# One PSUM tile each for the turned last rows of k and of q, in place of one tile that both share

## The chip, the core and the metric

The kernel runs on one core of a Trainium2 chip. Its five engines work side by side: TensorE (PE) multiplies matrices and turns tiles, VectorE (DVE) and ScalarE (ACT) move results out of PSUM and do the elementwise work, GpSimd (POOL) helps with copies and integer sums, and SyncE (SP) issues DMA transfers. The metric is the device time in microseconds (us). The kernel before takes 1052.27 us, the median of 3 runs (1051.37 to 1053.14).

## What is computed

Three parts follow one another: attention with a memory term, a gated layer, and a second gated layer on its output. Batch, heads, rows and depth are 4, 8, 576 and 64; the gated layers have 2304 rows, width 512 and inner width 1536.

```python
def _attn_ref(q, k, v, M_prev, z_prev, beta):
    scores = scale * np.matmul(q, k.transpose(0, 1, 3, 2))
    scores = np.where(causal, -1000000000.0, scores)
    a = np.exp(scores - scores.max(-1, keepdims=True))
    a /= a.sum(-1, keepdims=True) + 1e-09
    local = np.matmul(a, v)
    q_p = phi(q)                       # elu(q) + 1
    mem_out = einsum(q_p, M_prev) / (einsum(q_p, z_prev) + 1e-06)
    return g * mem_out + (1 - g) * local        # g = sigmoid(beta)

def _moe_ref(x, w_gate, w_val, w_out):
    return (sigmoid(x @ w_gate) * (x @ w_val)) @ w_out

def _moe2_ref(x, w_a, w_b, w_out):
    return ((x @ w_a) * (x @ w_b)) @ w_out
```

## The kernel before

Attention works on pairs of heads: 16 pairs, p = 0 to 15. The 576 rows of a pair are cut into five blocks, the first of 64 rows and four of 128. The blocks form two groups, X (0, 2, 3) and Y (1, 4). For each pair PE turns k and q, so that depth lies on the partitions (`turn` for the first 448 columns, CUT, and `turn4` for the last 128), multiplies them (`scores`, L233), and then turns the exponentials and the mixed tiles (`turn_w` at L368, `turn_mix` at L380) and multiplies them with v (`pv`, L398 and L404). DVE takes the maxima of the scores (L262), ACT the exponentials (L267). From pair 9 on (PARTS) the turned k and q are kept as a high and a low part, and a score takes three products.

PE also works on the first gated layer: while the attention of batch 1 and later batches is computed, the gated layer of the batch before runs in single products of three matmuls each (`mm3`, L484 to L486), which the loop places between the steps of attention (step `M`). The weights come in by DMA and are unpacked on the way (L438 to L454, steps `W`). After the attention, the rest of the gated layers runs as one dense stretch of matmuls on PE.

PSUM has eight banks. Four hold the scores (`psa`). A pool of three, `pst`, serves in turn all the turned tiles and the outputs of `pv`: every call of `tp()` takes the next of its three buffers. Up to pair 4 each fourth call takes a fourth bank instead (`psx`); from then on this bank belongs to the gated layer (`psm`). So a tile of `tp()` can be written only when the tile that had the same bank three calls before has been copied out. In one turn of the loop the calls come in a written order (`FIRST`, `FIFTH` and `LATER`): of that order the steps `m0`, `m1`, `mY` (mixed tiles), `wA` (two tiles, one per head), `t4` (`turn4`), and in the next turn `pvX`, `pvY`, `wB` and `wC` matter here. The copies out of the `wA` tiles are made on ACT (L152, names `aw<-tp`, 128x512).

Only the order within some steps is pinned; else the framework places each instruction on its engine by its own estimate of times. So a change of the tiles can move instructions on all engines. The turned last rows of k are copied out by ACT (L176, `kt`), those of q by DVE (L173, `qt`); from pair 9 on both are copied by ACT (L167) and then by DVE (L168).

Of the kernel before, what the change touches and what calls it, by code (L numbers as in the profile page):

```python
# [19 lines left out]
def kernel(  # L20
# [17 lines left out]
    P = 128  # L38
    B, H, S, D = q.shape
# [8 lines left out]
    CUT = 448  # L48
# [105 lines left out]
    def tp():  # L154

        turns[0] += 1
        return (psx if psm is None and turns[0] % 4 == 0 else pst).tile([P, 512], F32, tag="tp", name="tp")


    def put(p, key, src, a, z):  # L160
        if a == 0:
            st[key, p] = at.tile([P, 2, S], F32, tag=f"{key}t", name=f"{key}t")
        t = st[key, p][:, 0, a:z]
        scale = -1.0 / D ** 0.5 if key == "q" else 1.0
        if p >= PARTS:
            h, l = (st[key, p][:, i, a:z].bitcast(F32R) for i in H2)
            act.activation(out=h, in_=src, func=AF.Copy, scale=scale)  # L167
            r = vec.scalar_tensor_tensor(  # L168
                out=l, in0=src, scalar=scale, in1=t, op0=ALU.mult, op1=ALU.subtract
            )  # L170
            return r
        elif key == "q":
            return vec.tensor_scalar(  # L173
                out=t, in0=src, scalar1=scale, scalar2=None, op0=ALU.mult
            )
        return act.activation(out=t, in_=src, func=AF.Copy)  # L176

    def turn1(out, p, key, i):
        src = st[f"{key}n", p][:, i].rearrange("p h d -> p (h d)")
        pe.transpose(out=out, in_=src, identity=ident)  # L180

    def begin():


        idle, tk, tq = tp(), tp(), tp()

        def spin(n):
            for _ in range(n):
                pe.matmul(
                    idle[:, 0:P], lhsT=tws[0], rhs=tws[1], start=True, stop=True,  # L190
                    skip_group_check=True,
                )

        act.activation(out=early, in_=tws[0][:, 0:2], func=AF.Exp)
        spin(5)
        turn1(tk[:, 0:P], 0, "k", 0)
        turn1(tq[:, 0:P], 0, "q", 0)
        spin(4)
        for key, t in (("q", tq), ("k", tk)):
            for i in (1, 2, 3):  # L200
                turn1(t[:, C03[i]:C03[i] + P], 0, key, i)
            st["first", key] = put(0, key, t[:, 0:CUT], 0, CUT)
        turn4(0)
# [5 lines left out]
        put(p, key, t[:, 0:CUT], 0, CUT)  # L209

    def turn4(p):
        t = tp()
        for c, key in enumerate("kq"):
            turn1(t[:, c * P:(c + 1) * P], p, key, 4)
        for c, key in enumerate("kq"):
            put(p, key, t[:, c * P:(c + 1) * P], CUT, S)

    def scores(p, blocks):

# [401 lines left out]
    if True:  # L621
# [89 lines left out]
        def one(step, p):  # L711
# [27 lines left out]
            elif step == "phi1" and new:  # L739
                if not p:  # L740
                    load_z(0)
                phi1(p)
            elif step == "phi2" and new:
                phi2(p)
            elif step == "lv" and new:
                load_v(p)
            elif step == "lz" and nx:
                load_z(nx)
            elif step in ("tk", "tq") and nx:
                turn(nx, step[1])  # L750
            elif step == "t4" and nx:
                turn4(nx)
            elif step in ("m0", "m1", "mY") and old is not None:
                turn_mix(old, step[1])
            elif step == "M":
                M()
            elif step == "Mo" and old is not None:
                M()
            elif step == "S":
                settle()  # L760
            elif step == "sp":
                split(1)
            elif step == "W":
                if p >= 1:
                    for _ in range(1 if p < 4 else 2):
                        w_next()
# [50 lines left out]
    with tc.manual_schedule(engines={mybir.EngineType.PE}):  # L817
# [46 lines left out]
        for c in range(MA):  # L864
            for kind in range(3):
                t = ws[0, c, kind]
# [869 lines left out]
```

## Time and profile before

| | |
|---|---|
| median of 3 runs | 1052.27 us (1051.37 to 1053.14) |
| profiled execution | 1050.67 us |
| its span, first to last instruction | 1048.8 us |
| PE busy | 1026.1 us, 98% |
| DVE busy | 736.2 us, 70% |
| ACT busy | 589.7 us, 56% |
| POOL busy | 188.6 us, 18% |
| mean granted TensorE clock | 0.998 |

The profiled execution's time is 1.9 us over its span, and 1.6 us under the median of the runs. A matmul's busy time overlaps that of the next, so the step from one start to the next is what it costs: a row "x12" in a timeline stands for twelve in a row, with the start of the first. "[0.98 <-PE tp L368]" behind a row says that the engine was idle for 0.98 us before it and that the release came from PE's line 368. The first 120 us, where attention runs alone or with little beside it, have nearly all of PE's idle time up to the end of attention.

### The profile page before, as it was taken

How to read it: one execution, taken by the hardware profiler on the slowest of the kernel's cores; microseconds unless marked ns; L12 is line 12 of the kernel's file. 1: busy time of each engine (PE TensorE's matmuls, PEld its weight loads, DVE VectorE, ACT ScalarE, POOL GpSimd, SP SyncE). 2: the span in 40 equal slices, each digit the busy share in tenths (PEclk: the TensorE clock that was granted, in tenths of full speed). 3: DMA queues.
4: the chain of work that ended last, by engine and by line, in shares of the span. 5: the costliest groups of instructions: out<-in, count | busy, mean ns of one | idle time of the engine just before them, and what ended most of it. 6: DMA issues, size and time to landing. Idle time of an engine off the chain costs nothing.

```text
span 1048.8 us, 17727 instructions
## 1 busy us (share of the span) xinstructions
PE 1026.1 (98%) x6158; PEld 858.6 (82%) x6158; DVE 736.2 (70%) x1590; ACT 589.7 (56%) x1276; POOL 188.6 (18%) x204
## 2 busy tenths in 40 slices
PE   7988999999999999999999999999999999999998
PEld 5656777777878987888888889888888888899998
DVE  6888755665627797765587558686586676898885
ACT  7888867867836556445654335454444545453442
POOL 3544521331211111111211000221121311000000
PEclk9999999999999999999999999999999999999999
DMA  7665434233215424332378754444362575644441
GB/s 174 157 182 159 136 90 127 77 87 85 59 55 172 161 86 145 103 128 80 118 247 300 241 170 161 131 136 136 96 190 91 188 232 183 216 142 146 137 141 61
DMA packets 154697, 150.14 MB, mean 143 GB/s; under 512 B 74608, under 2 KB 112624, under 8 KB 154608
## 3 DMA queue, kind: packets, MB, share of 16 engines
q1 hardware_dynamic: 152560, 148.16, 45.8%
q8 instruction: 48, 0.79, 0.3%
q10 hardware_dynamic: 2048, 0.86, 0.3%
q14 instruction: 41, 0.34, 0.1%
HBM read 103.29 MB, written 45.69 MB: 142 GB/s over the span
## 4 chain that ended last, share of the span: by engine, by line
PE 79%; DVE 7%; ACT 5%; DMA 5%; issue 2%; POOL 1%; SPq 1%; ACTq 0%; DVEq 0%; POOLq 0%
PE gv L486 17%; PE gv L485 17%; PE gv L484 17%; PE gv L1474 10%; PE m L484 3%; PE m L486 3%; PE m L485 3%; PE tp L404 2%; PE sc L233 2%; PE tp L368 2%; ACT s L267 2%; PE tp L398 1%; PE tp L380 1%; ACT aw L152 1%; DMA st<-in_moe_w_b_dram 1%
## 5 line engine op out<-in xcount | busy, mean ns | idle before, releaser
L484 PE MATMUL gv<-xm,w 128*128 128x512 f32 (+1 forms) x752 | 272.4, 362 | 0.5 <-ACT ev L1207 0.4
L486 PE MATMUL gv<-xm,w 128*128 128x512 f32 (+1 forms) x752 | 272.6, 363 | 0.0
L485 PE MATMUL gv<-xm,w 128*128 128x512 f32 (+1 forms) x752 | 272.6, 363 | 0.0
L925 POOL TENSOR_TENSOR wt<-wt,st 128x512 int32<-128x512 int32 x60 | 84.3, 1408 | 496.1 <-DVE wt L921 356.9
L484 PEld LDWEIGHTS gv<-xm,w 128*128 128x128 f32 x752 | 141.4, 188 | 23.8 <-ACT ev L1207 1.3
L485 PEld LDWEIGHTS gv<-xm,w 128*128 128x128 f32 x752 | 141.5, 188 | 22.6
L486 PEld LDWEIGHTS gv<-xm,w 128*128 128x128 f32 x752 | 141.6, 188 | 22.0
L1207 ACT ACTIVATE ev<-gv 128x512 f32<-128x512 f32 (+1 forms) x172 | 93.8, 562 | 76.2 <-PE gv L486 58.0
L1211 DVE TENSOR_TENSOR ev<-gv,ev 128x512 f32<-128x512 f32 x120 | 80.9, 684 | 63.0 <-PE gv L486 31.8
L1474 PE MATMUL gv<-wo,gs 128*128 128x256 f32 x1008 | 120.8, 282 | 0.1
L1474 PEld LDWEIGHTS gv<-wo,gs 128*128 128x128 f32 x1008 | 120.3, 190 | 0.7 <-DVE gs L1447 0.5
L152 ACT ACTIVATE aw<-tp 128x512 f32<-128x512 f32 (+2 forms) x144 | 69.0, 507 | 46.3 <-PE tp L368 32.5
L262 DVE CUSTOM_DVE_ANT_0 s<-sc,mask 128x64 f32<-128x64 f32 (+4 forms) x160 | 69.0, 484 | 21.7 <-PE sc L233 21.6
L915 ACT ACTIVATE wt<-st 128x512 f32<-128x512 f32 x60 | 39.7, 668 | 73.5 <-DMA st<-in_moe_w_out_dram 30.7
L1446 ACT ACTIVATE gs<-ev 128x512 fp32r<-128x512 f32 (+1 forms) x96 | 51.1, 572 | 52.7 <-DMA ev<-gd 25.1
L267 ACT ACTIVATE s<-s,mx 128x320 f32<-128x320 f32 (+3 forms) x128 | 77.3, 607 | 2.7 <-DVE mx L262 2.7
L916 ACT ACTIVATE st<-st 128x512 int32<-128x512 uint32 x60 | 40.2, 669 | 39.5 <-DMA st<-in_moe_w_gate_dram 14.3
L486 PE MATMUL gv<-gs,w 128*128 128x512 f32 (+1 forms) x160 | 59.6, 373 | 0.0
L485 PE MATMUL gv<-gs,w 128*128 128x512 f32 (+1 forms) x160 | 59.4, 371 | 0.0
L233 PE MATMUL sc<-kt,qt 64*128 64x320 f32 (+4 forms) x468 | 55.8, 367 | 3.4 <-DVE mx L262 2.9
L484 PE MATMUL gv<-gs,w 128*128 128x512 f32 (+1 forms) x160 | 58.9, 368 | 0.0
L1447 DVE TENSOR_TENSOR gs<-ev,gs 128x512 fp32r<-128x512 f32 (+1 forms) x96 | 56.0, 617 | 3.3 <-ACT gs L1446 3.2
(159 smaller groups left out, 1825.7 us busy)
## 6 DMA issues: line engine op xcount, KB each, us to landing
gd<-ev SPq DMA_DIRECT2D x80, 256.0 KB
ev<-gd SPq DMA_DIRECT2D x80, 256.0 KB
st<-in_moe_w_out_dram SPq DMA_DIRECT2D x24, 512.0 KB
st<-in_moe_w_gate_dram SPq DMA_DIRECT2D x12, 512.0 KB
st<-in_moe_w_val_dram SPq DMA_DIRECT2D x12, 512.0 KB
st<-in_moe_w_a_dram SPq DMA_DIRECT2D x12, 512.0 KB
st<-in_moe_w_b_dram SPq DMA_DIRECT2D x12, 512.0 KB
x<-rd SPq DMA_DIRECT2D x32, 144.0 KB
```

Of the source, the lines that this page charges most:

```text
L152: act.activation(out=out, in_=src, func=AF.Copy)
L233: st["anchor"] = pe.matmul(scs[e][:, SC0[i] + a:SC0[i] + z], lhsT=x, rhs=y, start=n == 0, stop=n == len(terms) - 1, skip_group_check=True,)
L262: st["pace"] = vec.tensor_tensor_reduce(out=s, in0=scs[e][:, SC0[i]:SC0[i] + w], in1=mask[:, c:c + w], scale=1.0, scalar=BIG, op0=ALU.add, ...
L267: st["apace"] = act.activation(out=o, in_=s, func=AF.Exp, scale=-1.0, bias=mx[:, i:i + 1], accum_out=sms[p % 2][:, i:i + 1, e],)
L484: pe.matmul(o, lhsT=w[:, 0, ws_], rhs=xh, start=first, stop=False, skip_group_check=True)
L485: pe.matmul(o, lhsT=w[:, 0, ws_], rhs=xl, start=False, stop=False, skip_group_check=True)
L486: return pe.matmul(o, lhsT=w[:, 1, ws_], rhs=xh, start=False, stop=last, skip_group_check=True)
L925: pool.tensor_tensor(out=c32, in0=c32, in1=lo, op=ALU.add)
L1207: act.activation(out=t[:, 0:n], in_=src[:, 0:n], func=func)
L1211: st["gate"] = vec.tensor_tensor(out=t, in0=src, in1=t, op=ALU.add)
L1447: vec.tensor_tensor(out=t[:, 1, 0:n], in0=f[:, 0:n], in1=t[:, 0, 0:n].bitcast(F32), op=ALU.subtract,)
L1474: st["gate"] = pe.matmul(o, lhsT=t[:, th, q_], rhs=w[:, wl_, wc:wc + 256], start=first and (ends_ or not r) and not z, stop=last and (ends ...
```

## The change

`turn4` takes two tiles of `tp()` in place of one. Before, the turns of k and of q went side by side into columns 0 to 255 of one tile, and both copies followed. Now k is turned and copied, and then q from a tile of its own.

```diff
     def turn4(p):
-        t = tp()
-        for c, key in enumerate("kq"):
-            turn1(t[:, c * P:(c + 1) * P], p, key, 4)
-        for c, key in enumerate("kq"):
-            put(p, key, t[:, c * P:(c + 1) * P], CUT, S)
+        for key in "kq":
+            t = tp()
+            turn1(t[:, 0:P], p, key, 4)
+            put(p, key, t[:, 0:P], CUT, S)
```

The number of matmuls, copies and transfers is the same; a turn of the loop takes 16 tiles of `tp()` in place of 15. Line numbers below `turn4` are one lower after the change (L232 for L233, L397 for L398).

On PE, around the start of pair 2, the kernel before turns the last rows of pair 2, multiplies the first half of pair 0's output, and only then comes to the scores of pair 2 (`sc`); `kn` and `qn` are the rows of k and q, `aw` the copied tiles:

```order
L180 MATMUL tp<-ident,kn 128x128
L180 MATMUL tp<-ident,qn 128x128
L398 MATMUL tp<-aw,mv 64x320 x2
L404 MATMUL tp<-aw,vn 64x256 x4
L404 MATMUL tp<-aw,vn 64x128 x2
L368 MATMUL tp<-ident,s 128x128 x4
L233 MATMUL sc<-kt,qt 128x64 x2
L233 MATMUL sc<-kt,qt 128x320 x2
L233 MATMUL sc<-kt,qt 128x448 x2
```

The changed kernel has at the same place:

```order
L367 MATMUL tp<-ident,s 128x128 x4
L232 MATMUL sc<-kt,qt 128x64 x2
L232 MATMUL sc<-kt,qt 128x320 x2
L232 MATMUL sc<-kt,qt 128x448 x2
L180 MATMUL tp<-ident,qn 128x128
L397 MATMUL tp<-aw,mv 64x320
L180 MATMUL tp<-ident,kn 128x128
L397 MATMUL tp<-aw,mv 64x320
L403 MATMUL tp<-aw,vn 64x256 x4
L403 MATMUL tp<-aw,vn 64x128 x2
```

The scores have moved ahead of the output matmuls, and the turns of the last rows behind the scores. (The scores of group X don't need the last rows.)

On ACT, in pair 6, `aw` are the copies of the turned exponentials, `sg` is the first sigmoid, `mix` the first exponentials of the pair, and `ACT_TABLE_LOAD` changes the function table. The order before is:

```order
L152 ACTIVATE aw<-tp 128x512
L530 ACT_TABLE_LOAD
L530 ACTIVATE sg<-sg 128x1024
L267 ACT_TABLE_LOAD
L267 ACTIVATE mix,sm_93<-s_1355,mx 128x64
L267 ACTIVATE mix,sm_93<-s_1358,mx 128x64
L152 ACTIVATE aw<-tp 128x512
L453 ACTIVATE w_1340<-wt 128x512
L267 ACTIVATE s,sm_93<-s,mx 128x320
L152 ACTIVATE aw<-tp 128x512
```

And after the change:

```order
L152 ACTIVATE aw<-tp 128x512
L529 ACT_TABLE_LOAD
L529 ACTIVATE sg<-sg 128x1024
L452 ACTIVATE w_1347<-wt 128x512
L152 ACTIVATE aw<-tp 128x512
L176 ACTIVATE kt<-tp 128x128
L266 ACT_TABLE_LOAD
L266 ACTIVATE mix,sm_93<-s_1362,mx 128x64
L266 ACTIVATE mix,sm_93<-s_1365,mx 128x64
```

The last copy of the two `wA` tiles, and that of k's last rows, have moved ahead of the second table load. On DVE a piece earlier, at pair 5, three operations have moved ahead of the first maxima, behind which they stood: the subtraction of a second weight piece (L454), the scaling of the next (L438) and `qp` (L287).

On PE in the later pairs, here where the first half of a pair's output begins at 176.66 us in the trace of before, the order before is:

```order
L180 MATMUL tp<-ident,kn 128x128
L180 MATMUL tp<-ident,qn 128x128
L484 MATMUL m<-xs,w_794 128x512
L485 MATMUL m<-xs,w_794 128x512
L486 MATMUL m<-xs,w_794 128x512
L484 MATMUL m<-xs,w_794 128x512
L485 MATMUL m<-xs,w_794 128x512
L486 MATMUL m<-xs,w_794 128x512
L398 MATMUL tp<-aw,mv 64x320 x2
```

And after the change:

```order
L180 MATMUL tp<-ident,kn 128x128
L483 MATMUL m<-xs,w_798 128x512
L484 MATMUL m<-xs,w_798 128x512
L485 MATMUL m<-xs,w_798 128x512
L483 MATMUL m<-xs,w_798 128x512
L484 MATMUL m<-xs,w_798 128x512
L485 MATMUL m<-xs,w_798 128x512
L180 MATMUL tp<-ident,qn 128x128
L397 MATMUL tp<-aw,mv 64x320 x2
```

The turn of q's last rows has moved behind six matmuls of the gated layer, directly ahead of the output matmuls. From pair 6 on this is all that moves on PE, while on ACT and DVE nothing moves any more from about 110 us on.

## Rows read from the trace of the kernel before

**Rows 1.** Busy time by stretch: window, length, busy per engine, PE clock, DMA share, GB/s.

```profile
10.00:70.00 60.00, 49.65 (x394) 34.58 (x396) 51.30 (x169) 55.35 (x166) 26.71 (x38) 0.99 0.70 169
70.00:120.00 50.00, 46.24 (x319) 33.22 (x318) 40.74 (x113) 40.78 (x99) 25.00 (x26) 0.98 0.56 157
...
170.00:200.00 30.00, 30.00 (x232) 22.95 (x230) 15.14 (x50) 23.95 (x56) 7.44 (x11) 1.00 0.34 89
```

**Rows 2.** Waits by pair, whole span: engine and line, releaser, us in total, times, longest.

```profile
DVE qt L173 <- ACT kt L176: 3.8, 3, 1.6
```

**Rows 3.** Timeline of DVE: start, length, engine, line, operation, names, shapes, idle before.

```profile
30.06 0.49 DVE L410 TENSOR_TENSOR x<-tp,x 128x320 f32<-128x320 f32 x1 [1.25 <-DMA x<-rd]
...
31.80 0.21 DVE L262 CUSTOM_DVE_ANT_0 s<-sc,mask 128x64 f32<-128x64 f32 x1
...
44.11 0.29 DVE L173 TENSOR_SCALAR qt<-tp 128x128 f32<-128x128 f32 x1 [1.34 <-ACT kt L176]
...
72.62 0.22 DVE L262 CUSTOM_DVE_ANT_0 s<-sc,mask 128x64 f32<-128x64 f32 x1
```

**Rows 4.** Timeline of ACT in the first 100 us, same columns.

```profile
28.67 1.09 ACT L152 ACTIVATE aw<-tp 128x512 f32<-128x512 f32 x2 [0.98 <-PE tp L368]
29.64 0.63 ACT L453 ACTIVATE w<-wt 128x512 fp32r<-128x512 f32 x1
32.06 0.35 ACT L267 ACTIVATE mix<-s,mx 128x64 f32<-128x64 f32 x1 [1.78 <-DVE mx L262]
...
43.83 0.25 ACT L176 ACTIVATE kt<-tp 128x128 f32<-128x128 f32 x1
...
73.83 0.63 ACT L453 ACTIVATE w<-wt 128x512 fp32r<-128x512 f32 x1 [2.42 <-POOL wt L450]
...
93.01 1.28 ACT L267 ACT_TABLE_LOAD   x1
...
94.98 0.57 ACT L152 ACTIVATE aw<-tp 128x512 f32<-128x512 f32 x1
```

**Rows 5.** Timeline of PE, same columns.

```profile
26.21 0.76 PE L398 MATMUL tp<-aw,mv 128*64 128x320 f32 x4 [0.68 <-ACT aw L152]
...
28.57 1.78 PE L233 MATMUL sc<-kt,qt 64*128 64x64 f32 x12
...
69.25 3.32 PE L233 MATMUL sc<-kt,qt 64*128 64x64 f32 x12
...
95.61 0.76 PE L398 MATMUL tp<-aw,mv 128*64 128x320 f32 x4 [1.45 <-ACT aw L152]
```

**Rows 6.** Granted clock on PE: window, length, busy (instructions), clock, DMA share, GB/s.

```profile
66.00:68.00 2.00, 1.09 (x8) 1.00 0.66 105
...
69.00:72.00 3.00, 3.00 (x14) 0.50 0.32 112
```

**Rows 7.** Timeline of ACT at two later pairs, columns as in rows 3.

```profile
174.65 0.58 ACT L152 ACTIVATE aw<-tp 128x512 f32<-128x512 f32 x1
175.24 1.28 ACT L267 ACT_TABLE_LOAD   x1
...
177.22 0.57 ACT L152 ACTIVATE aw<-tp 128x512 f32<-128x512 f32 x1
...
258.24 0.57 ACT L152 ACTIVATE aw<-tp 128x512 f32<-128x512 f32 x1
```

**Rows 8.** Timeline of PE at later pairs, columns as in rows 3.

```profile
145.60 0.27 PE L340 MATMUL tp<-ident,tw 128*128 128x128 f32 x1
145.62 0.48 PE L485 MATMUL m<-gl,w 128*128 128x512 f32 x1
...
176.66 0.76 PE L398 MATMUL tp<-aw,mv 128*64 128x320 f32 x4
...
257.69 0.76 PE L398 MATMUL tp<-aw,mv 128*64 128x320 f32 x4
```

**Rows 9.** Waits of PE from 96 us to the end, columns as in rows 2.

```profile
PE gv L484 <- ACT sg L547: 0.8, 1, 0.8
```

## Prediction, made before the changed kernel ran

> **What bounds the kernel now.** I read the busy time by stretch first. Between 10 and 70 us no engine is full, but ACT (55.35 us of 60) and DVE (51.30) are nearer to it than PE (49.65) [rows 1]: here the chain through ACT and DVE sets the pace, and PE idles for 60 - 49.65 = 10.35 us. From 70 to 120 us PE idles for another 3.76 us, and at 170 to 200 us it is busy for 30.00 us of 30 [rows 1]. So there are two regimes. Early, a microsecond saved on ACT or DVE can bring PE forward; late, only time on PE counts, and every wait of PE stays to the end. The waits of PE after 96 us show how little slack there is: the largest one from outside attention is 0.8 us [rows 9], and it follows PE's own work, so it gives nothing back.
>
> Then I read what the shared tile costs, by pairs of waits: DVE's copy of q's last rows waits for ACT's copy of k's last rows for 3.8 us in all, in three places [rows 2]. At 43.83 us ACT copies k for 0.25 us, and DVE, idle for 1.34, starts its copy at 44.11 [rows 3, 4]. Both read one tile, in different columns, and don't overlap.
>
> **What the change removes.** These waits: q's copy has a tile of its own and needs only PE. [...]
>
> **What it moves early.** The extra tile changes the framework's estimate, and with it the order up to about 110 us. Two moves matter.
>
> At pair 2 the scores now come ahead of the output matmuls. Before, scores began at 28.57, behind matmuls that had begun at 26.21 [rows 5]; DVE sat idle for 1.25 us until 30.06 at the output's product and reached the first maximum at 31.80, and ACT idled 0.98 and 1.78 us up to 32.06 [rows 3, 4]. At most 0.98 + 1.78 = 2.76 us can be had. With the new order and the old durations, DVE's maxima need not wait for the product. ACT's copies, the phi exponential and the weight copy (29.64, [rows 4]) end at about 29.6, so that the mix exponentials start some 2.4 us earlier; pair 1 gives back about 0.2, since `qp` now stands ahead of its maxima. I take a lead of 2.2 us at pair 2, bounds 0 and 2.76.
>
> At pair 5 the lead is spent. The first maxima stood at 72.62, behind one weight piece [rows 3]; now they stand behind the second as well, whose ACT copy is at 73.83 for 0.63 us [rows 4]. They can't begin before 73.83 + 0.63 = 74.46, plus three operations on DVE of about 0.6, 0.5 and 0.7 us (steps in the same timeline): some 76.3 less the lead, 1.5 us later than before if the lead is 2.2. About as much is hidden again: before, PE and ACT had idled there for other reasons (ACT 2.42 us ahead of 73.83). I put what is left of the lead behind pair 5 at 0.2 us, bounds -1.5 and +1.1.
>
> At pair 6 the order gains by itself. PE's output matmuls waited 1.45 us until 95.61 for ACT's copy at 94.98 [rows 4, 5]; so a bank comes free 95.61 - 94.98 = 0.63 us after the copy's start. That copy stood behind a table load at 93.01. In the new order the output needs the second of the two copies, but both stand ahead of that load: 93.01, plus about 0.53 for the weight copy that is put between (its step in the same timeline), plus 0.63, is 94.17, or 1.44 us earlier. Together: 1.44 + 0.2 = **1.6 us earlier** when PE becomes full, bounds -0.1 (1.44 less the 1.5 lost at pair 5) and 2.5 (1.44 + 1.1).
>
> **What it adds late.** Tiles take the three banks in turn. Before, the calls ran mY, wA (first head), wA (second), t4, pvX: pvX got the bank of the first wA tile. With two tiles for t4, q's turn gets that bank, and pvX gets that of the second wA tile, whose copy on ACT comes later. Behind pvX on PE are pvY, wB, wC and the gated layer's matmuls: all in one queue, nothing passes. So I compare, pair by pair, the second copy's start + 0.63 with the start of pvX. At the other pairs from 116 us on it is 1 us or more ahead (read in the same timelines). At two it isn't: a sigmoid with its table loads (1.28 us) sits between the copies.
> - 177.22 + 0.63 - 176.66 = 1.19 us [rows 7, 8]
> - 258.24 + 0.63 - 257.69 = 1.18 us [rows 7, 8]
>
> Before, the copy that mattered was at 174.65, long done [rows 7]. PE has nothing else to do in its order while it waits, and is full around it. Sum: **+2.4 us**. Bounds: 0, if ACT comes earlier by as much there, and 3.0, if ACT's chain behind the sigmoid slips by 0.3 at each. pvY and wB take over the banks of the copies of k's and q's last rows, which come about half a microsecond or more ahead of need in these pairs once pvX has waited. The turn of q that moves alone between matmuls costs nothing: the lone turn at 145.60 lets the next matmul start at 145.62 [rows 8].
>
> [...]
>
> **Sum.** The profiled execution took 1050.67 us, span 1048.8. 1050.67 + 2.4 - 1.6 = 1051.5. The median of the runs is 1052.27, that is 1.6 above the profiled execution, so on its scale 1052.27 + 0.8 = **1053.0 us**. About 0.2%, 2.1 us, is what a measurement of this kernel can tell from no change.
>
> **Rivals.**
> [...]
> - *Lead kept whole, late stalls absent.* 1052.27 - 2.4 = 1049.9. For: the early lead is 2.2 by the sum, and ACT has 6 us idle of 30 at 170 to 200 [rows 1]. Against: the late copies follow scores and sigmoid, so ACT's lead moves with PE's.
> - *Waits given back.* The 3.8 us of DVE waits [rows 2] come back in full in place of the order's gain: 2.4 - 3.8 = -1.4, 1050.9. Against: at 44.11 ACT was the fuller engine, and DVE's wait ends with ACT's work that had to be done anyway.
> - *Nothing reaches the end.* 1052.3: the stalls are hidden and so are the gains.
>
> **Chances.** Forecast 0.42 (of it 0.04 faster, 0.33 same, 0.05 slower); clock dip 0.28 (0.01 same, 0.27 slower); lead kept 0.13 (0.11 faster, 0.02 same); waits given back 0.10 (0.05 each faster and same); nothing 0.07 (same). That is faster 0.20, same 0.48, slower 0.32. The forecast's own range follows from its bounds: 0 to 3.0 less -0.1 to 2.5, of which both ends together are unlikely: 1051 to 1055. The range that holds eight in ten reaches to the rivals on both sides: 1049.5 to 1056.5.
>
> **What would show it.** In the trace of after: (1) no wait of DVE's q copy on ACT's k copy; (2) two waits of PE at the output's first matmul on ACT's copy, 1.2 us each, near 176 and 257 us; (3) scores of pair 2 near 26 us, and PE's wait near 94 us ended earlier than 95.61; (4) the clock between 66 and 85 us. The prediction is wrong if PE, once full, leads or lags by more than 3 us at 120 us, or if the two stalls aren't there.

## The result, and the profile after

The changed kernel takes **1059.68 us**, median of 6 runs (1057.34 to 1062.62), beside 1051.70 us for the kernel before (6 runs, 1051.07 to 1053.14): a ratio of 1.0072 [1.0057, 1.0088]. The prediction was 1053.0 with a range up to 1056.5, so it was wrong: the change costs 8.0 us, and 0.8 had been expected. Its profiled execution took 1060.85 us, span 1058.7, against 1050.67 and 1048.8. Lines of the changed kernel stand one lower than before (L397 is L398 of before).

Two views say where the time went. The first is a table worked out from the timelines of PE: how much later the second scores of a pair (the matmuls of 64x192, twelve, from pair 9 on eighteen) begin than in the trace of before, in us. This is called PE's lag.

```
pair      0     1     2     3     4     5     6     9    10    13    14    15
after  0.12  2.46  1.16  0.17  3.67  5.17  5.35  5.32  6.51  6.60  7.79  7.78
```

Up to pair 6 the change loses 5.35 us in this execution; two steps of 1.2 follow at pairs 10 and 14. What lies between 7.8 and the 10.2 us of the two executions comes after pair 15; 1.7 us of it are waits of single matmuls in the dense stretch, which differ from one trace to the next. The second view is the timeline of PE in the changed kernel, at the places that rows 5 and 8 show of before (columns: start, length, engine, line, operation, names, shapes, count, idle before):

```profile
21.23 1.09 PE L180 MATMUL tp<-ident,qn 128*128 128x128 f32 x4 [1.99 <-ACT kt L176]
...
27.12 1.78 PE L232 MATMUL sc<-kt,qt 64*128 64x64 f32 x12
...
45.42 0.55 PE L367 MATMUL tp<-ident,s 128*128 128x128 f32 x3
45.90 0.65 PE L397 MATMUL tp<-aw,mv 128*64 128x256 f32 x4
...
57.09 2.63 PE L232 MATMUL sc<-kt,qt 64*128 64x64 f32 x12
...
73.28 3.06 PE L232 MATMUL sc<-kt,qt 64*128 64x64 f32 x12
...
79.36 0.65 PE L397 MATMUL tp<-aw,mv 128*64 128x256 f32 x4 [0.88 <-ACT kt L176]
...
100.97 0.76 PE L397 MATMUL tp<-aw,mv 128*64 128x320 f32 x4
...
183.17 0.76 PE L397 MATMUL tp<-aw,mv 128*64 128x320 f32 x4 [1.08 <-ACT aw L152]
...
265.47 0.76 PE L397 MATMUL tp<-aw,mv 128*64 128x320 f32 x4 [1.08 <-ACT aw L152]
```

The scores of pair 2 begin at 27.12, 1.45 us before the 28.57 of [rows 5]: the early lead came, at the first scores. At the second scores of the same pair PE is 1.16 us behind (table). The scores of pair 5 begin at 73.28 and not at 69.25, and the output of pair 6 begins at 100.97, 5.36 later than the 95.61 there, though it waits for nothing any more. At pair 5 a wait is new: the second half of the output, at 79.36, waits 0.88 us for ACT's copy of k's last rows; before it did not wait there. The two late waits are there, at 183.17 and 265.47, each 1.08 long; before, the same matmuls ran without a wait [rows 8]. In the list of waits of PE from 100 us on they head the list, and the one of [rows 9] stands unchanged behind them:

```profile
PE tp L397 <- ACT aw L152: 2.2, 2, 1.1
...
PE gv L483 <- ACT sg L546: 0.8, 1, 0.8
```

DVE's wait for ACT's copy of k's last rows, 3.8 us in [rows 2], is gone; the waits of the same operation for PE's turns rose from 4.9 to 6.5 us. By stretch (columns as in rows 1):

```profile
10.00:70.00 60.00, 50.86 (x377) 35.87 (x376) 47.72 (x160) 52.39 (x158) 24.81 (x35) 0.94 0.66 166
...
170.00:200.00 30.00, 28.92 (x208) 22.99 (x208) 17.00 (x53) 23.79 (x57) 7.97 (x13) 1.00 0.25 68
```

From 10 to 70 us PE is busy for longer than in [rows 1] (50.86 against 49.65 us) with fewer matmuls (377 against 394): its clock was 0.94 there and had been 0.99. At 170 to 200 it idles for 1.08 us, the late wait; before for none.

The order that moved shows best on DVE at pair 3. After the change, in DVE's timeline (with pairs 1 and 5 around it):

```profile
18.43 0.82 DVE L286 SCALAR_TENSOR_TENSOR qp<-qn,e 128x640 f32<-128x640 f32 x1 [1.27 <-POOL mix L325]
19.18 0.22 DVE L261 CUSTOM_DVE_ANT_0 s<-sc,mask 128x64 f32<-128x64 f32 x1
...
44.48 0.83 DVE L286 SCALAR_TENSOR_TENSOR qp<-qn,e 128x640 f32<-128x640 f32 x1 [1.06 <-ACT e L283]
45.23 0.22 DVE L261 CUSTOM_DVE_ANT_0 s<-sc,mask 128x64 f32<-128x64 f32 x1
...
46.71 0.49 DVE L409 TENSOR_TENSOR x<-tp,x 128x320 f32<-128x320 f32 x1
...
49.13 0.42 DVE L409 TENSOR_TENSOR x<-tp,x 128x256 f32<-128x256 f32 x1
50.63 0.86 DVE L502 TENSOR_TENSOR xs<-x,xs 128x512 fp32r<-128x512 f32 x1 [1.08 <-ACT xs L152]
...
52.24 0.35 DVE L261 CUSTOM_DVE_ANT_0 s<-sc,mask 128x192 f32<-128x192 f32 x1
...
79.65 0.81 DVE L286 SCALAR_TENSOR_TENSOR qp<-qn,e 128x640 f32<-128x640 f32 x1
80.38 0.21 DVE L261 CUSTOM_DVE_ANT_0 s<-sc,mask 128x64 f32<-128x64 f32 x1
```

And in the kernel before, DVE's timeline at pair 1 (first line) and in the same stretch of pair 3:

```profile
17.11 0.16 DVE L262 CUSTOM_DVE_ANT_0 s<-sc,mask 128x64 f32<-128x64 f32 x1
...
44.32 0.21 DVE L262 CUSTOM_DVE_ANT_0 s<-sc,mask 128x64 f32<-128x64 f32 x1
...
45.56 0.82 DVE L287 SCALAR_TENSOR_TENSOR qp<-qn,e 128x640 f32<-128x640 f32 x1
46.30 0.87 DVE L410 TENSOR_TENSOR x<-tp,x 128x320 f32<-128x320 f32 x2
...
48.44 0.68 DVE L503 TENSOR_TENSOR xs<-x,xs 128x512 fp32r<-128x512 f32 x1
49.81 0.36 DVE L262 CUSTOM_DVE_ANT_0 s<-sc,mask 128x192 f32<-128x192 f32 x1
```

with its PE:

```profile
45.01 0.60 PE L398 MATMUL tp<-aw,mv 128*64 128x256 f32 x4
46.63 1.53 PE L368 MATMUL tp<-ident,s 128*128 128x128 f32 x12
...
54.05 1.78 PE L233 MATMUL sc<-kt,qt 64*128 64x64 f32 x12
```

Before, PE multiplied both halves of the output (second half at 45.01) and then made the twelve turns of the steps `wB` and `wC` (46.63); DVE multiplied both halves into x in one go (46.30, x2), and after 2 us came `xs`, then the second maxima at 49.81. After, three turns of `wB` stand between the halves (45.42, 45.90): the halves are parted. DVE multiplies the first half in at 46.71, takes two maxima and two steps of a weight piece, and multiplies the second in only at 49.13; ACT's part of `xs` comes later, DVE waits 1.08 us for it, a weight piece (L453) that stood behind the second maxima now stands ahead of them, and they begin at 52.24. The first scores of pair 4 go from 54.05 to 57.09. `qp`, behind the first maxima before, stands ahead of them at pairs 1, 3 and 5.

The granted clock of PE (columns as in rows 6) fell in three places, and was 0.50, as at 69 to 72 us before [rows 6], in parts of them (22 to 24, 56 to 58 and 73 to 75 us):

```profile
21.00:24.00 3.00, 2.77 (x12) 0.55 0.89 197
55.00:58.00 3.00, 2.82 (x15) 0.57 0.13 43
...
72.00:75.00 3.00, 2.65 (x14) 0.58 0.29 104
```

### The profile page after: what moved, and what is told of

Read it like the earlier page. It is cut to its first block, busy times and chain, and to the rows that moved or that the text cites. A ratio compares the mean times of both kernels' runs of the same rounds, so it can differ in the third digit from the quotient of the medians.

```text
span 1058.7 us, 17727 instructions
## 1 busy us (share of the span) xinstructions
PE 1031.9 (97%) x6158; PEld 862.3 (81%) x6158; DVE 735.8 (69%) x1590; ACT 591.3 (56%) x1276; POOL 188.6 (18%) x204
## 4 chain that ended last, share of the span: by engine, by line
PE 81%; DVE 6%; ACT 4%; DMA 4%; issue 2%; POOL 1%; SPq 1%; ACTq 0%; DVEq 0%; POOLq 0%
PE gv L485 17%; PE gv L484 17%; PE gv L483 17%; PE gv L1473 10%; PE sc L232 3%; PE tp L403 3%; PE m L483 3%; PE m L485 3%; PE m L484 3%; PE tp L367 2%; PE tp L397 2%; PE tp L379 1%; ACT s L266 1%; PE tp L180 1%; DMA st<-in_moe_w_b_dram 1%
## 5 line engine op out<-in xcount | busy, mean ns | idle before, releaser
L152 ACT ACTIVATE aw<-tp 128x320 f32<-128x320 f32 (+2 forms) x144 | 69.3, 508 | 50.6 <-PE tp L367 35.7
L232 PE MATMUL sc<-kt,qt 64*128 64x320 f32 (+4 forms) x468 | 58.5, 376 | 2.2 <-DVE mx L261 1.8
```

The costliest lines, as they stand in the source:

```text
L152: act.activation(out=out, in_=src, func=AF.Copy)
L232: st["anchor"] = pe.matmul(scs[e][:, SC0[i] + a:SC0[i] + z], lhsT=x, rhs=y, start=n == 0, stop=n == len(terms) - 1, skip_group_check=True,)
```

## The experiments

Each was timed against the kernel before on the same chip; a ratio carries its 95% interval. "Later at pair n" is the figure of the table above, from one profiled execution. In executions that leave the first pairs as they were (e2, e11) that figure is 1.6 and 1.1 us at pair 6, in e13 2.2, so a difference of one or two microseconds there says little without the medians. A hold makes the framework place an operation behind another one. Lines of kernels that hold both forms of `turn4` stand six higher than before's.

**e1, the two tiles at pairs 0 to 6 only.**

```diff
     def turn4(p):
+        if p < 7:
+            for key in "kq":
+                t = tp()
+                turn1(t[:, 0:P], p, key, 4)
+                put(p, key, t[:, 0:P], CUT, S)
+        else:
+            t = tp()
...
```

The branch behind `else` is the old body. Of the kernels that follow with this form only the condition is shown.

> The two tiles for pairs below 7 only, the shared tile from pair 7 on. Its order up to 110 us is that of the changed kernel. Theory (the loss has two parts, an early one from the order and a late one from the two waits for the second copy): the early part alone, about 5.4 us over the kernel before, and no wait of PE near 183 and 265 us. Rival A (the loss sits in the late pairs, and the early difference is only where the profile happened to land): within 1.5 us of the kernel before. Rival B (the extra tile costs a little at every pair): about 3 us over.

1057.64 against 1052.98 us, 1.0048 [1.0036, 1.0060]. From pair 6 on the lag stays at 7.1 us (its profiled execution, 1060.64, is its longest); no late wait. The early part costs 4.7 us by the medians, and should have gained 1.6.

**e2, at pairs 7 to 15 only.**

```diff
+        if p >= 7:
```

> The shared tile for pairs below 7, two tiles from pair 7 on. Its order up to 110 us is that of the kernel before. Theory: only the two late waits, 1.1 to 1.2 us each, so 2.2 to 2.4 us over the kernel before. Rival A (the loss sits late): 7 to 8 us over. Rival B (each pair pays): about 4 us over.

1054.66 against 1052.98, 1.0020 [1.0011, 1.0030]. PE's lag grows by 1.18 at pair 10 and by as much at pair 14, and from pair 6 on nowhere else by more than 0.15.

**e11, at pairs 10 and 14 alone.**

```diff
+        if p in (10, 14):
```

> Two tiles at pairs 10 and 14 only, the two at which the second wA copy is late; all orders up to 110 us as before. Theory: the whole of the late loss, 2.2 us over the kernel before (two waits of 1.1 us on PE). Rival (the late loss is spread over the pairs from 7 on): under 0.7 us.

1054.34 against 1051.39, 1.0021 [1.0011, 1.0031]: a second tile at two pairs of sixteen makes the whole late cost. The waits of PE from 100 us on:

```profile
PE tp L404 <- ACT aw L152: 2.2, 2, 1.1
```

**e3 and e4, `qp` held behind the maxima at every pair, with two tiles (e3) and with the shared one (e4).** Both to see whether `qp` alone is the early loss.

```diff
-        with tc.issue_after(st["pace"].ins) if not p else ExitStack():
+        with tc.issue_after(st["pace"].ins):
```

> The changed kernel with two tiles everywhere, and qp (the last step of phi on DVE) held behind the first maxima of its pair in every pair, not in pair 0 alone. Theory (qp ahead of the maxima at pairs 1, 3 and 5 makes DVE wait for POOL and ACT, the maxima come late and PE pauses into a lower clock): the early loss goes, the late waits stay: 1.5 to 3.5 us over the kernel before, first matmuls of pair 6's output within 1.5 us of 95.6. Rival (the extra tile in the four, later three, banks costs early on whatever the order): 5 us or more over, with PE waiting for copies at pairs 1 to 5 as in the changed kernel.

> The kernel before (shared tile) with the same hold on qp. Control for the hold itself. In the kernel before qp stood ahead of the maxima at pair 2 and inside them at pair 3. Theory: within 1.5 us of the kernel before. Rival (the hold by itself is worth several us, so that the run with two tiles and the hold says nothing of the tiles): 3 us or more faster or slower.

1065.07 against 1052.98, 1.0122 [1.0106, 1.0138], and 1068.84, 1.0153 [1.0135, 1.0171]. The control missed: the hold itself costs 16 us with the shared tile; it also binds pairs whose order had not moved. With this hold two tiles are 3.8 us faster than one, on another order again. So e3 says nothing of the tiles in the changed kernel, and later holds were put only where the order had moved.

**e5 to e7, e1 with `qp` held at pair 1 (e5), at pair 3 (e6), at both (e7).**

The edit of e7 (`hold` is the third maximum; e6 has it with 0 and 3, and e5 holds behind `pace`, the last maximum, with 0 and 1; pair 0 is held in the kernel before too):

```diff
+                if blocks is X_ and (i, e) == (2, 0):
+                    st["hold"] = st["pace"]
...
-        with tc.issue_after(st["pace"].ins) if not p else ExitStack():
+        with tc.issue_after(st["pace" if not p else "hold"].ins) if p in (0, 1, 3) else ExitStack():
```

> As e1 (two tiles below pair 7), with qp of pair 1 alone held behind that pair's first maxima, where it stands in the kernel before. At pair 5 the three operations then also come back behind the first maxima by themselves; pair 3 keeps qp ahead. Theory (the early loss comes from what stands ahead of the first maxima at pairs 1, 3 and 5): 2 to 3 us less than e1, 2 to 3 us over the kernel before; second scores of pair 1 near 20 us and no lower clock at 21 to 25 us. Rival (e3 and e4 show that a hold on qp costs time by itself, whatever the pair): 6 us or more over.

> As e1, with qp of pair 3 alone put behind the third of that pair's maxima, as in the kernel before; eight rows of DVE move, two of PE. Theory: the first maxima of pair 3 come 1 to 1.8 us earlier than in e1, scores of pair 4 follow by as much, and e6 is 1 to 2.5 us faster than e1 (2.5 to 4 us over the kernel before). Rival (pair 3's delay is in ACT's and DVE's weight pieces, not in qp): as e1 within 0.7 us.

> As e1, with qp where the kernel before has it at pairs 1, 3 and 5, and two tiles. Theory (the operations ahead of the first maxima, not the tiles, make the early loss): within 1.5 us of the kernel before, on either side. Rival (the extra tile takes a bank that the early pairs lack): 3 us or more over, with PE waiting for copies at pairs 1 to 5.

1055.58, 1.0034 [1.0022, 1.0046]; 1055.64, 1.0029 [1.0019, 1.0040]; 1055.33, 1.0028 [1.0015, 1.0042], all against 1052.54. `qp` would carry 1.5 to 2 us of e1's 4.7 (the intervals still touch e1's), and the rest stays: e7 loses it between pair 3 (0.52 later) and pair 4 (2.77). The theory that `qp` is all of it fell. In all three the halves of pair 3's output stay parted; in e5 and e7 DVE's order at pair 5 is that of before again.

**e8, at pairs 7 to 15 q's tile taken after `pvX`, so that no copy of `wA` is waited for.**

```diff
     def turn4(p):
+        if p >= 7:
+            return half4(p, "k")
         t = tp()
...
+    def half4(p, key):
+        t = tp()
+        turn1(t[:, 0:P], p, key, 4)
+        put(p, key, t[:, 0:P], CUT, S)
...
+                if 7 <= p < NP:
+                    half4(p, "q")
```

> As e2 (two tiles from pair 7 on), but the tile of q's last rows is taken behind the output's first half in place of ahead of it, so that the output takes the first wA tile's bank again and q's turn the second's. As many tiles as e2. Theory (the late loss is the wait for the second wA copy by the bank's turn): the two waits of 1.1 us go; within 0.7 us of the kernel before, 1.5 to 2.4 us faster than e2. Rival (a tile more per pair costs, whichever bank it takes): as e2, 1.7 to 2.4 us over.

1063.12 against 1052.54, 1.0097 [1.0084, 1.0110]. The waits on `aw` went, two on DVE's copy of k came (1.3 us), and much else moved on PE, and q's turns now stand between the halves of the output. PE is later by 0.66 us at pair 6 and by 11.4 at pair 15. So it doesn't tell one tile more from another order, and where these 10 us come from is left open.

**e9, pairs 0 to 3 only, and e10, pairs 4 to 6 only.**

```diff
+        if p < 4:
```

```diff
+        if 4 <= p < 7:
```

> Two tiles for the pairs below 4 only (where four banks serve the turned tiles), the shared tile from 4 on. Its order on PE, DVE and ACT is nearly that of e1. Theory (the early loss is in the order that the tiles of pairs 1 to 3 bring about): 3.5 to 5 us over the kernel before, as e1. Rival (it is the fall from four banks to three, at pairs 4 to 6): within 1.5 us of the kernel before.

> Two tiles for pairs 4, 5 and 6 only. Up to pair 5 the order is that of the kernel before; from there the gated layer's matmuls stand behind the turns and mixes, and the copies of pair 6 ahead of the table load, as in the changed kernel. Theory: the step that the prediction counted as a gain at pair 6, 1.4 us, comes here if DVE isn't late at pair 5: 0.5 to 1.5 us faster than the kernel before. Rival (three banks for a tile more are too few): 1.5 to 4 us over.

1056.84 against 1051.39, 1.0045 [1.0030, 1.0060], and 1052.77, 1.0012 [1.0002, 1.0022]. The second tiles of the pairs up to 3 are enough for the early loss, though their order reaches further: PE's lag in e9 goes from 1.63 at pair 4 to 4.71 at pair 5. And pairs 4 to 6, where the prediction had its 1.44 us of gain, lose 1.2, little more than the noise: PE's timeline of e10 says why.

```profile
75.19 0.65 PE L404 MATMUL tp<-aw,mv 128*64 128x256 f32 x4 [1.60 <-ACT kt L176]
...
85.47 0.52 PE L386 MATMUL tp<-ident,mix 128*128 128x128 f32 x3 [1.61 <-POOL wt L456]
...
87.73 0.48 PE L490 MATMUL m<-xs,w 128*128 128x512 f32 x1
...
91.10 1.78 PE L239 MATMUL sc<-kt,qt 64*128 64x64 f32 x10
...
96.84 0.76 PE L404 MATMUL tp<-aw,mv 128*64 128x320 f32 x4
```

The output of pair 6 comes 96.84 - 91.10 = 5.74 us behind the first scores, where it was 95.61 - 89.04 = 6.57 before: 0.83 us of the 1.44 are there, a part of them because four turns that stood behind the scores now stand ahead. But the scores come 2.06 late, because the gated layer's matmuls stand behind the turns and mixes now (87.73), and PE waits 1.61 us where they had run. At pair 5 the second half of the output waits 1.60 us for ACT's copy of k (75.19); before it didn't wait (74.54). In the kernel before, PE's timeline has these places here:

```profile
74.54 0.60 PE L398 MATMUL tp<-aw,mv 128*64 128x256 f32 x4
...
83.07 0.48 PE L484 MATMUL m<-xs,w 128*128 128x512 f32 x1
...
88.46 0.66 PE L380 MATMUL tp<-ident,mix 128*128 128x128 f32 x4 [1.26 <-DVE qt L173]
89.04 1.78 PE L233 MATMUL sc<-kt,qt 64*128 64x64 f32 x12
```

**e12 and e15, the two tiles only where no order moves early and no late copy follows.** e12 has pair 6, e15 does not.

```diff
+        if p in (3, 4) or p >= 6 and p not in (10, 14):
```

```diff
+        if p in (3, 4) or p >= 7 and p not in (10, 14):
```

> Two tiles at pairs 3 and 4 and from 6 on, without 10 and 14: the pairs at which the framework's order hardly moves (PE four rows, DVE two, ACT none in the first 200) and no late copy stands in the way; shared at 1, 2, 5, 10 and 14. Theory (the tiles themselves cost and give nothing; the moved order early and the two late copies cost): within 0.7 us of the kernel before. Rival A (each tile more costs bank time): 2 us or more over. Rival B (the waits of DVE that go are worth their time): 1.5 us or more faster.

> As e12 without pair 6, where the second wA copy is late too (96.52 + 0.63 us against an output that began at 95.61, so 1.5 us): two tiles at pairs 3, 4, 7, 8, 9, 11, 12, 13 and 15. Theory (second tiles cost nothing where neither the order moves nor the wA copy is late): within 0.7 us of the kernel before. Rival (each costs): 1.5 to 3 us over.

e12: 1055.44 against 1051.39, 1.0037 [1.0021, 1.0052], a miss. PE's timeline shows a wait of the late kind at pair 6, though its tiles at pairs 10 and 14 are shared:

```profile
97.75 0.76 PE L404 MATMUL tp<-aw,mv 128*64 128x320 f32 x4 [1.21 <-ACT aw L152]
```

and ACT's timeline of e12 the copy behind it:

```profile
93.61 1.28 ACT L273 ACT_TABLE_LOAD   x1
...
95.58 0.57 ACT L152 ACTIVATE aw<-tp 128x512 f32<-128x512 f32 x1
...
97.13 0.57 ACT L152 ACTIVATE aw<-tp 128x512 f32<-128x512 f32 x1
```

97.13 + 0.63 = 97.76: the rule of the prediction (the second copy's start + 0.63) holds to 0.01 us at a pair for which it had foreseen no late wait, since the order that moves this copy ahead of the table load isn't there. e15, without that pair: 1053.02 against 1052.73, 0.9999 [0.9990, 1.0008]. With a second tile at nine pairs DVE's wait on k's copy falls from the 3.8 us of [rows 2] to this, while its waits for PE's turns rise from 4.9 to 6.4, and the time is the same:

```profile
DVE qt L173 <- ACT kt L176: 0.9, 1, 0.9
```

**e13, the shared tile, but the count that sends each fourth tile to the fourth bank up to pair 4 moved on by one at each `turn4`; and e14, two tiles at pair 2 alone.**

```diff
             put(p, key, t[:, c * P:(c + 1) * P], CUT, S)
+        turns[0] += 1
```

```diff
+        if p == 2:
```

> The kernel before with the shared tile everywhere and no tile more; only the count of tiles, which sends each fourth one to the fourth bank up to pair 4, is moved on by one per pair, as the second tile would. DVE's order then takes the same moves at pairs 2 and 3 as in the changed kernel (the output's second product and the split of x behind the second maxima, qp of pair 3 ahead of the maxima); qp of pair 1 stays behind. Theory (the early loss is the moved order at pairs 2 to 5 and needs no second tile): 2 to 4 us over the kernel before. Rival (the second tile itself costs, by its turn in the banks): within 1 us of the kernel before.

> Two tiles at pair 2 only. DVE's order at pairs 2 and 3 moves as in the changed kernel, pairs 1 and 5 stay as before. Theory: one tile more is enough to move the order at pairs 2 and 3, and the time is that of e13 and e5 within 1 us: 2 to 4 us over the kernel before. Rival (the loss grows with the number of second tiles, three in e9): a third of e9, 1 to 1.7 us.

e13: 1053.55 against 1052.73, 1.0007 [0.9998, 1.0016]: the theory of 2 to 4 us missed. In its trace the scores of pair 2 do stand ahead of the output (26.58) and `qp` of pair 3 ahead of the maxima (43.40), as in the changed kernel, but the halves of pair 3's output stay together. So those two moves, and which tiles the fourth bank gets, are not the loss; of a second tile's turn in the banks it says nothing. e14: 1056.36, 1.0028 [1.0013, 1.0044]: one tile more in one pair makes over half of the early loss by the medians. In its trace PE is 0.73 us ahead at pair 3 and 4.0 behind at pair 4, with the halves of the output parted as in the changed kernel, and loses no more than 0.2 behind it. Its granted clock there (columns as in rows 6):

```profile
55.00:60.00 5.00, 5.00 (x21) 0.50 0.48 111
```

**e16 and e17, `wB` of pair 3 held behind the last matmul of the output's second half: e16 is the changed kernel, e17 is e1, each with this hold.**

```diff
-                with pinned(pin):
+                with pinned("P" if step == "wB" and p == 3 else pin):
```

> The changed kernel, two tiles everywhere, with one hold: at pair 3 the turns of wB come behind the last matmul of the output's second half, as in the kernel before, and not between its halves. DVE's order at pair 3 then has the second product and the split of x ahead of the maxima again, the weight piece behind them, and pair 5 comes back by itself. Theory (the early loss is the chain at pair 3: output's second half late on PE, its product late on DVE, the split of x late on ACT and DVE, the next maxima late): the early part falls from 4.7 to 0 to 1.5 us and the late part stays: 2.2 to 3.7 us over the kernel before. Rival (something else of the new order): 5 us or more over.

> The same hold in e1 (two tiles below pair 7 only). Theory: 0 to 1.5 us over the kernel before, 3 to 4.5 us faster than e1; second scores of pair 4 within 1.5 us of 61.2. Rival: 3.5 us or more over.

1056.68 against 1052.16, 1.0040 [1.0028, 1.0052], and 1054.23, 1.0025 [1.0015, 1.0034]. Both come out above their theory, e16 by less than its interval. The hold gives back some 3.4 us in the one (1.0072 to 1.0040) and 2.4 in the other (1.0048 to 1.0025). It brings back DVE's order at pair 5 as well, with the first maxima ahead of the second weight piece. DVE's timeline of e17, with `qp` still ahead:

```profile
44.36 0.82 DVE L293 SCALAR_TENSOR_TENSOR qp<-qn,e 128x640 f32<-128x640 f32 x1 [1.06 <-ACT e L290]
...
46.54 0.81 DVE L416 TENSOR_TENSOR x<-tp,x 128x320 f32<-128x320 f32 x2
...
49.99 0.36 DVE L268 CUSTOM_DVE_ANT_0 s<-sc,mask 128x192 f32<-128x192 f32 x1
```

Both halves are multiplied into x in one go again, the second maxima come at 49.99 (before 49.81, changed 52.24), and PE is 0.25 us later at pair 4 and 0.09 ahead at pair 5. Then it loses 2.6 up to pair 6, where e10 loses 1.2, here with a lower clock as well (0.69 at 85 to 90 us, where the kernel before has 1.00). It has e10's waits at pairs 5 and 6. PE's timeline of e17:

```profile
75.03 0.65 PE L404 MATMUL tp<-aw,mv 128*64 128x256 f32 x4 [1.60 <-ACT kt L176]
...
85.31 0.52 PE L386 MATMUL tp<-ident,mix 128*128 128x128 f32 x3 [1.61 <-POOL wt L456]
...
98.15 0.76 PE L404 MATMUL tp<-aw,mv 128*64 128x320 f32 x4
```

**e18, e17 with `qp` held as in e7 beside it.**

```diff
+        with tc.issue_after(st["pace" if not p else "hold"].ins) if p in (0, 1, 3) else ExitStack():
...
+                with pinned("P" if step == "wB" and p == 3 else pin):
```

> The hold of e17 and those of e7 on qp together, two tiles below pair 7. Everything that stood ahead of the first maxima at pairs 1, 3 and 5 is back where it was, and scores of pair 2 stay ahead of the output matmuls. Theory: the lead at pair 2 that the prediction counted on can now be kept: 0 to 2 us faster than the kernel before. Rival (the lead is lost to other waits, as all leads before it): within 1.5 us of the kernel before.

1054.90 against 1052.16, 1.0025 [1.0016, 1.0035]: no better than e17, and neither the theory nor its rival came. The lead of pair 2 is not kept (1.24 later at pair 3, 3.64 at pair 5, where the output's second half waits 2.84 us for ACT's copy of k). None of the versions beat the kernel before.

## Why the prediction was wrong, step by step

**What bounds the kernel**: held. From pair 6 on the lag of PE changes by 1.2 us at pairs 10 and 14 each and hardly elsewhere, so what these two waits (1.08 us each) cost stays. Early, time comes and goes: e7, e14 and e17 gain and lose by microseconds from one pair to the next.

**What the change removes**: the wait went, and gave nothing (e15, 0.9999). The rival "waits given back" is refuted: of the 2.9 us that went in e15, 1.5 came back as a wait of the same copy for PE's turn of q (at the place of the longest, 1.58 us at 136.36 before, DVE then waits 1.57 for PE), and the rest made nothing shorter.

**What it adds late**: right. 2.4 us were predicted; the profile shows two waits of 1.08, e2 costs 0.20% and e11 0.21%, some 2.1 us each. The mechanism is shown by e11, and again by e12 at pair 6. Where nothing else moved, a second tile neither gained nor lost (e15, 0.9999), and with three banks in turn it brought PE a wait of 1.08 us at each of pairs 10 and 14 and of 1.21 at pair 6 (e12).

**What it moves early**: the step that failed. -1.6 us was predicted, +4.7 measured (e1). Its parts:
- *Pair 2.* A lead of 2.2 was taken; the first scores came 1.45 earlier, the second 1.16 later. The move gained about what was said (2.46 late at pair 1, 0.17 at pair 3), but pair 1 had lost as much, and in no trace here is PE more than 0.8 us ahead of before at any pair. One reading was wrong: DVE's 1.25 us until 30.06 ended, by the row itself, with a transfer (`<-DMA x<-rd`) and not with PE's matmuls.
- *Pair 1.* `qp` ahead of the maxima was put at 0.2 us. The maxima went from 17.11 to 19.18, 2.1 later, since `qp` waited 1.27 for POOL first, and PE waited 1.99 at 21.23. By pair 3 this was made up for.
- *Pair 3 has no term at all.* "Two moves matter", the prediction said, and went from pair 2 to pair 5. There 3.5 us were lost (0.17 late at pair 3, 3.67 at pair 4): turns of `wB` between the halves of the output, the second half multiplied in late, `xs`, a weight piece and the second maxima behind it, and a dip of the clock (0.57 at 55 to 58 us). In the seven traces that part the halves (after, e1, e5, e6, e7, e9, e14) PE loses 1.6 to 4.7 us between these two pairs; with the halves together it loses at most 0.1 (e8, e10 to e13, e15 to e18), in e2 1.0. e3 and e4 are left out, as their hold moves every pair. e14 has this loss alone and costs 2.9 us; e17 puts the halves together, has pair 5's order back with it, and gets 2.4 us. This is the largest part of the error.
- *Pair 5.* The first maxima were put at 76.3 less the lead; they came at 80.38. PE was 3.67 late at pair 4 already, so 1.5 of the 5.17 at pair 5 were made here. A wait without a term lies here too. The prediction saw that `pvY` and `wB` take over the banks of the copies of k's and q's last rows, and compared them in the later pairs only. At pair 5 the output's second half then waits for ACT's copy of k: 0.88 us in the changed kernel, 1.60 in e10, e16 and e17, 2.84 in e18, 3.12 in e6, 3.48 in e1, and in none of the kernels that share the tile at pair 5. (In e5 and e7, whose profiled executions had a mean clock of 0.996, PE comes there later and it is absent.) What it costs in the end is open: in e10 the lag at pair 5 is 0.07 in spite of it.
- *Pair 6.* The gain of 1.44 was sized from PE's wait for the copy alone. In e10, 0.83 of it shows, and the same reordering takes 2.06 from the scores ahead of it, because the matmuls that had filled PE's waits stand elsewhere. The forecast has no term for that.

**The clock dip**, with 0.28 in the chances, was nearer than the forecast. Before, PE was busy for 1.09 us of 2 at 66 to 68 us and the clock was 0.50 at 69 to 72 [rows 6]; the twelve scores took 3.32 us at 69.25 and 1.78 at 28.57 [rows 5]. By these rows one such dip is estimated at 3.32 - 1.78 = 1.54 us; with the late waits, and with the early gain taken by late maxima, that is 1052.27 + 2.4 + 1.54 = 1056.2, just under the range's upper end and nearer to the result than any time in the prediction. But in the changed kernel dips came at three places and not at one (0.55 at 21 to 24, 0.57 at 55 to 58, 0.58 at 72 to 75 us), and they are not all of it. Among 113 executions of the kernel before the mean granted clock was 0.9992, among the six of the changed kernel 0.9963. Over 81 executions of the ten kernels here that have two tiles at pair 2 (e3 left out), an execution is on average 0.6 us longer than its kernel's mean for each 0.001 of clock below its kernel's mean; by this the dips go with (3.67 - 0.78) x 0.6 = 1.7 of the 8.0 us, and by the six executions of the changed kernel alone (1.2 us for 0.001) with 3.5. In e14 the five executions at 0.996 or less took 1058.6 us in the mean, the seven at 0.998 or more 1054.3. This is a correlation: no run here sets the clock and leaves the order. And e6, 3.1 us slower than the kernel before, shows no dip in its trace (1.00 at 20 to 25, 55 to 60 and 70 to 75 us, 0.999 over the execution). So of the 8.0 us the two late waits cost 2.2, and 5.8 are lost early, to the moved order, the waits at pair 5 and the dips; the dips may be 1.7 to 3.5 of it, and that split stays open.

**The chances.** "Slower" had 0.32, and it came. The text itself called a lead or lag of over 3 us at 120 us its refutation; the lag was 5.35. The range left out that an order that moves at every pair from 1 to 6 can lose at each; pairs 2, 5 and 6 were worked out, pair 1 was put at 0.2, and the sum was taken as if the others cost nothing. The time of the rival "lead kept whole" takes off 2.4 us where the lead was put at 2.2; nothing here hangs on it.

## What to carry to other kernels

Where a scheduler places the work, an edit of a buffer changes the order, and the order can be worth more than the buffer (here 4.7 us in e1, none in e15): go through every place that moves while no engine is full, ask at each what the moved work had been filling, and give the ones not worked out a bound in the range. With three banks in rotation one more tile shifted here who waits for whom (1.08 us at pairs 10 and 14): compare each write with the copy out of the bank's last holder, on the trace, for every tile behind the new one and at every pair. And the waits that ended with another engine's needed work were no time to be had: 2.9 us of them went in e15, and the ratio is 0.9999.

## What the runs showed of the hardware

After a pause of PE of the same length the clock fell in one run and not in another. In e10 and in e17 PE waited 1.61 us for the same piece of POOL's, at 85.47 and 85.31. In e17 the clock then fell to 0.50:

```profile
87.00:89.00 2.00, 1.84 (x7) 0.50 0.59 213
```

In e10 it stayed at 1.00 all through:

```profile
84.00:92.00 8.00, 5.74 (x35) 1.00 0.43 138
```

In the changed kernel the dip at 21 to 24 us (0.55) stands behind a wait as well, of 1.99 us until 21.23. But in these runs the wait alone does not foretell a dip: in e17 PE also waits 1.60 us until 75.03, and the clock is 1.00 from 75 to 86 us; in e6 it waits 3.12 us there, and the mean clock of that execution is 0.999. The twelve executions of e14 have mean clocks from 0.995 to 1.000 and times from 1052.15 to 1059.79 us. So how often a kernel's executions dip has to be read from many of them, and one profile can mislead by several microseconds.
